# Two-pass products for the half-filled block of an MLP's width, in an fp32 kernel built from three-pass matmuls

## The chip, the cores and the metric

The kernel runs on one core of a Trainium2 chip. TensorE (PE; its weight loads are PEld) multiplies from SBUF into eight PSUM banks; VectorE (DVE) and ScalarE (ACT) read PSUM and SBUF; GpSimd (POOL) issues DMAs and does small copies and fills; SyncE (SP) issues DMAs. Each of them works through its own queue in order, and semaphores hold an instruction until what it needs is done. The metric is the time of one execution on the device, in microseconds.

## The reference

```python
xn = layernorm(x)                                              # x: 2048 tokens x 640 channels
a, b = xn @ hid_re.T, xn @ hid_im.T
fnet = seq_re @ a - seq_im @ b                                 # 2048 x 2048 matrices
h = layernorm(xn)
u = gelu(einsum("bsd,sf->bdf", h, w1) + b1)                    # F = 1728
mlp = einsum("bdf,fs->bds", u, w2) + b2                        # transposed to tokens x channels
return x + fnet + mlp
```

All arrays are fp32. The MLP runs over the tokens: the first product ("up") sums over 2048 tokens and gives 1728 rows, the second ("down") sums over these 1728 and gives 2048 rows, both 640 columns wide.

## The kernel before

**Three passes.** An fp32 operand is cut into a high and a low part (type fp32r): ScalarE rounds it (`high`, L132), VectorE subtracts (`low`, L135). `three` (L141) multiplies high x high, high x low and low x high into one bank: three matmuls, lines L144, L145 and L146 of the profile. Low x low is left out.

**Seven products.** Large products are done two block rows at a time (a row pair) by a scheme of Strassen's kind: a 2 x 2 block matrix A11, A12, A21, A22 of weights, times 2 x 2 blocks of the moving operand, in seven products P1, P5, P6, P2, P7, P3, P4 (in this order, `order` in `row_steps`, L701) instead of eight. The moving operand's seven sums and differences are made once (`moving_of`, L594) and stay in SBUF, high and low; each has 320 columns. For the weights, VectorE makes, for each row pair, s = A21 + A22, then A21 := A11 - A21, A11 := s - A11, and A12 := A12 - A11 (`sums_of`). P1 takes the old A11, P5 takes s, P6 the new A11, P2 the old A12, P7 the new A21, P3 the new A12, P4 takes A22. Seven products are seven steps; a step's weights are a *piece*.

**The stages.** After the Fourier part's products over the tokens and over the channels come four stages of this kind:

- up 0 and up 1: each sums over half of the tokens (four quarters q of 128 per block), in seven row pairs r = 0 to 6. Pair r holds the blocks r and r + 7 of the 1728 rows. Block 13 has only 64 rows (`TAIL`); the host fills it with a second copy of them. Up 0 puts its results into a DRAM tensor `up`; up 1 gets them back with an accumulating DMA (L804), adds bias and applies GELU (L809).
- down 0 and down 1: the sums over the blocks 0 to 3 with 7 to 10, and 4 to 6 with 11 to 13 (three quarters q). Each has eight row pairs of the 2048 rows; results are accumulated onto the output by POOL's DMAs (`collect`, L783). In the second half of block 13 the moving operand is zero (L814).

A step of the up stages and of down 0 is 4 x 3 matmuls, one of down 1 is 3 x 3, all of 128 x 320.

**The order.** `turn_of` (L931) writes each turn: DMA loads; reads of the PSUM bank of the last step; sums of the weights; the high part of the piece for the step three turns on; jobs (making the moving operands); the low part of that piece; then the matmuls of this turn's step. Four places for pieces take turns, so a high part waits for the matmuls of four steps before. The banks are handed out in turn: P1, P6, P7 and P4 add into bank "z", P5 and P3 into "y", P2 into "w". After each product the bank is read: the first time copied by ScalarE (L767), later added to SBUF by VectorE (L761). In up 1 the reads of P2 and P7 go *aside* (L825): ScalarE copies, and a DMA of POOL's accumulates onto `up`, before L804 reads it back.

Of the kernel before, what the change touches and what calls it, by code (L numbers as in the profile page):

```python
# [8 lines left out]
F32 = mybir.dt.float32  # L9
# [5 lines left out]
P = 128  # L15
# [51 lines left out]
def fnet_plus_mixer(  # L67
# [70 lines left out]
    def sub(to, a, b):  # L138
        nc.vector.tensor_sub(to, a, b)  # L139

    def three(psum, w, m, first, last):  # L141

        (wh, wl), (mh, ml) = w, m
        nc.tensor.matmul(psum, wh, mh, start=first, stop=False, skip_group_check=True)  # L144
        nc.tensor.matmul(psum, wh, ml, start=False, stop=False, skip_group_check=True)  # L145
        nc.tensor.matmul(psum, wl, mh, start=False, stop=last, skip_group_check=True)  # L146
# [14 lines left out]
    def cut_place(j, n):  # L161

        if n > CH:
            turn, width = (j - s_hid) % 3, 2 * n
        else:
            turn, width = (j - s_hid if j < s_hid else j - s_up + 3) % 4, 2 * CH
        return cut[:, turn * width : turn * width + 2 * n].rearrange("p (a n) -> p a n", a=2)

    def cut_piece(source, n):
# [12 lines left out]

        return top, bottom
# [515 lines left out]
        return raws[k][:, raw_turn[k], :n]  # L699

    def row_steps(  # L701
        stage, nq, load_piece, at, end, bias=(None, None), base=None, earliest=0, each=None, aside=None,
    ):


        s0, n = len(steps), nq * P
        raw, banks, held = {}, {}, {}

        def load(*names):
            for name in names:  # L710
                raw[name] = raw_slot(n)
                load_piece(raw[name], int(name[1]) - 1, int(name[2]) - 1)

        def first_sum():
            k = n if n == D else CH
            raw["s"] = raws[k][:, raws[k].shape[1] - 1, :n]
            nc.vector.tensor_add(raw["s"], raw["A21"], raw["A22"])
# [10 lines left out]
        sums_of = (  # L728
            first_sum, lambda: sub(raw["A21"], raw["A11"], raw["A21"]),
            lambda: sub(raw["A11"], raw["s"], raw["A11"]), lambda: sub(raw["A12"], raw["A12"], raw["A11"]),  # L730
        )
        bank_of = {1: "z", 6: "z", 7: "z", 4: "z", 5: "y", 3: "y", 2: "w"}
        of_moving = {1: 0, 2: 1, 3: 2, 5: 3, 7: 4, 4: 5, 6: 6}

        goes_to = {1: (0, 0, True), 5: (1, 1, True), 6: (0, 1, True), 2: (0, 0, False), 7: (1, 1, False),
                   3: (0, 1, False), 4: (1, 0, True)}

        def products(i):
            def run(w):
                if i in (1, 5, 2):  # L740
                    banks[bank_of[i]] = bank()
                for q in range(nq):
                    ks = slice(q * P, (q + 1) * P)
                    m = moving[stage, q]
                    three(
                        banks[bank_of[i]][:, :H2], (w[0][:, ks], w[1][:, ks]),
                        (m[:, 0, of_moving[i], :], m[:, 1, of_moving[i], :]), i in (1, 5, 2) and q == 0, q == nq - 1,
                    )
            return run

        def read(i):
            def run():
                if i == 1:
                    held["c"] = place[at]()
                row, half, fresh = goes_to[i]
                cols = slice(half * H2, (half + 1) * H2)
                c, b = held["c"][:, row, cols], banks[bank_of[i]][:, :H2]
                if aside and i in (2, 7):
                    aside(i, row, half, b)
                elif not fresh:  # L760
                    nc.vector.tensor_add(c, b, c)  # L761
                elif base:
                    nc.vector.tensor_add(c, b, base()[:, row, cols])  # L763
                elif bias[row] is not None:
                    nc.scalar.activation(c, b, AF.Identity, bias=bias[row])
                else:
                    nc.scalar.activation(c, b, AF.Copy)  # L767
# [4 lines left out]
            return run  # L772

        for e, names in loads_of.items():
            loads[max(s0 + e, earliest)].append(lambda names=names: load(*names))
        for e, f in zip(sums_at, sums_of):
            sums[s0 + e].append(f)
        for e, i in enumerate(order):
            steps.append(cut_piece(lambda i=i: raw[operand[i]], n) + (products(i),))
            reads[s0 + e + 1].append(read(i))  # L780
        return s0

    def collect(c, ts):  # L783
# [10 lines left out]
        return row_steps("hid", ND, load_piece, ("ca", "cb")[n % 2], lambda c: collect(c, ts), earliest=earliest)  # L794

    def up(stage, r, at):
        def load_piece(to, i, j):
            nc.sync.dma_start(to, w1[r + NF2 * i, 2 * stage + j])

        def end(c):  # L800
            if stage == 0:
                nc.gpsimd.dma_start(part_up[r], c)
                return
            nc.gpsimd.dma_start(c, part_up[r], accum_op=ALU.add)  # L804

            def gelu(i):
                f = r + NF2 * i
                rows = P if f < NF else TAIL
                nc.scalar.activation(  # L809
                    c[:rows, i, :], c[:rows, i, :], AF.Gelu_apprx_tanh, bias=b1_sb[:rows, f : f + 1]  # L810
                )
                if rows < P:

                    nc.gpsimd.memset(c[rows:, i, :], 0.0)  # L814


            e = s0 + 7
            timed[e + 6].append(lambda: gelu(0))
            timed[e + 6].append(lambda: gelu(1))
            if r < 4:  # L820
                timed[e + 8].append(lambda: jobs.extend(moving_of("down0", r, f"slab{4 + r}", lambda: c)))
            else:
                timed[e + 8].append(lambda: nc.gpsimd.dma_start(part_up[r], c))

        def aside(i, row, half, b):  # L825

            t = place["x1"]()[:, r % 2, i // 7 * H2 : (i // 7 + 1) * H2]
            nc.scalar.activation(t, b, AF.Copy)
            nc.gpsimd.dma_start(part_up[r][:, row, half * H2 : (half + 1) * H2], t, accum_op=ALU.add)

        s0 = row_steps(
            f"up{stage}", 4, load_piece, at, end, earliest=s_up - 4, aside=aside if stage else None,
        )
        return s0

    def down(stage, t, at):
        f0, nq = (0, 4) if stage == 0 else (4, 3)
        ts = (t, t + NS // 2)
        last = stage == 1 and t == NS // 2 - 1

        def load_piece(to, i, j):
            f = f0 + NF2 * j
            nc.sync.dma_start(to, w2[ts[i], :, f * P : (f + nq) * P])

        def each(c, row, half, whole):
            if whole:
                nc.sync.dma_start(out_rows[ts[row]][:, half * H2 : (half + 1) * H2], c)

        held = []

        def before():

            held.append(place["v"]())
            for i in range(2):
                nc.sync.dma_start(held[0][:, i, :], out_rows[ts[i]])

        if last:
            loads[len(steps) - LOADS].append(before)
        bias = [b2_sb[:, i : i + 1] if stage == 0 else None for i in ts]
        return row_steps(  # L860
            f"down{stage}", nq, load_piece, at, lambda c: collect(c, ts), bias, (lambda: held[0]) if last else None,
            each=each if last else None,
        )


# [49 lines left out]
    timed[s_down + 14].append(lambda: jobs.extend(rests_hid[0] + [gets_hid[2]] + rests_hid[1] + rests_hid[2]))  # L915
    for t in range(NS // 2):
        down(1, t, ("ca", "cb")[t % 2])

# [87 lines left out]
```

## Time and profile before

| | us |
|---|---|
| three runs | 878.43, 878.82, 878.82 (median 878.82) |
| the profiled execution | 878.46 |
| its span, first to last instruction | 876.5 |
| up 0 / up 1 (about) | 529 to 614 / 614 to 700.2 |
| down 0 / down 1 (about) | 700.2 to 798.7 / 798.7 to 872.5 |

The span is from the first instruction to the last; the execution's own time is 2.0 us longer. Times within a trace count from the span's start. A row of the timeline is start, duration, engine, line, operation, tile written <- tiles read, shape; in brackets stands the idle time before it and what ended it. Matmuls overlap, so their rate is read from starts and not from durations. VectorE's and ScalarE's instructions overlap a little too: 512 columns take 0.68 us and follow each other every 0.60 us.

### The profile page before, as it was taken

The page shows a single profiled execution, that of the slowest core. Times are in us where ns is not written, and L with a number is a line of the kernel's source. Part 1 is how long each engine was busy: PE and PEld are TensorE (multiplying, and loading weights), DVE is VectorE, ACT ScalarE, POOL GpSimd, SP SyncE. Part 2 cuts the span into 40 slices and gives each one's busy share as a digit, 9 for nine tenths or more (in the row PEclk, how much of TensorE's full clock was granted, in tenths as well). Part 3 has the DMA queues.
Part 4 walks back from the last instruction along what each step waited for, and adds up shares of the span by engine and source line. Part 5 has one row for each costly group of instructions (what it writes and reads, how often), then busy time and mean ns, then how long its engine had stood idle before and what let it go on. Part 6 is the DMA issues. An engine that isn't in the chain of part 4 may idle for free.

```text
span 876.5 us, 13992 instructions
## 1 busy us (share of the span) xinstructions
PE 871.5 (99%) x4957; PEld 798.5 (91%) x4957; DVE 705.5 (80%) x1183; ACT 524.8 (60%) x956; POOL 123.3 (14%) x166
## 2 busy tenths in 40 slices
PE   9999999999999999999999999999999999999998
PEld 6888888888888888889999999999999999999998
DVE  7878878785888888587887788898689878886775
ACT  6656575754656555557555546675587756655553
POOL 0110100101121111122101101000112211111111
PEclk9999999999999999999999999999999999999999
DMA  7781644529294646769766765544677896756876
GB/s 272 229 291 49 213 195 149 212 84 346 38 252 62 191 88 162 178 99 205 165 138 150 155 176 159 192 146 150 147 153 169 196 276 139 179 126 131 161 160 129
DMA packets 85685, 147.14 MB, mean 168 GB/s; under 512 B 8432, under 2 KB 35568, under 8 KB 85360
## 3 DMA queue, kind: packets, MB, share of 16 engines
q1 hardware_dynamic: 64848, 95.56, 33.6%
q0 software_dynamic: 20624, 50.54, 29.8%
q8 instruction: 39, 0.64, 0.3%
q14 instruction: 30, 0.25, 0.1%
q10 hardware_dynamic: 144, 0.16, 0.1%
HBM read 99.63 MB, written 51.84 MB: 173 GB/s over the span
## 4 chain that ended last, share of the span: by engine, by line
PE 99%; DMA 0%; ACT 0%; DVE 0%; SPq 0%; issue 0%
PE psum L144 31%; PE psum L146 31%; PE psum L145 31%; PE psum L444 6%; DMA pieces<-in_dft_seq 0%; ACT piece L133 0%; ACT n L236 0%; DVE pair L763 0%; SPq L468 0%; DVE r L205 0%; DVE norm L209 0%; DVE r L203 0%; ACT q L197 0%; DVE norm L212 0%
## 5 line engine op out<-in xcount | busy, mean ns | idle before, releaser
L136 DVE TENSOR_TENSOR piece<-pieces,piece 128x512 fp32r<-128x512 f32 (+2 forms) x508 | 347.4, 688 | 132.8 <-ACT piece L133 127.7
L133 ACT ACTIVATE piece<-pieces 128x512 fp32r<-128x512 f32 (+2 forms) x508 | 317.3, 628 | 210.3 <-PE psum L146 71.9
L144 PE MATMUL psum<-piece,n 128*128 128x512 f32 x504 | 196.1, 389 | 0.0
L145 PE MATMUL psum<-piece,n 128*128 128x512 f32 x504 | 196.1, 389 | 0.0
L146 PE MATMUL psum<-piece,n 128*128 128x512 f32 x504 | 196.1, 389 | 0.0
L144 PE MATMUL psum<-sup,piece 128*128 128x320 f32 x392 | 121.1, 309 | 0.0
L145 PE MATMUL psum<-sup,piece 128*128 128x320 f32 x392 | 121.1, 309 | 0.0
L146 PE MATMUL psum<-sup,piece 128*128 128x320 f32 x392 | 121.1, 309 | 0.0
L144 PE MATMUL psum<-sdown,piece 128*128 128x320 f32 x392 | 121.1, 309 | 0.0
L145 PE MATMUL psum<-sdown,piece 128*128 128x320 f32 x392 | 121.1, 309 | 0.0
L146 PE MATMUL psum<-sdown,piece 128*128 128x320 f32 x392 | 121.1, 309 | 0.0
L139 DVE TENSOR_TENSOR pieces<-pieces 128x512 f32<-128x512 f32 (+3 forms) x142 | 112.3, 791 | 1.9
L145 PEld LDWEIGHTS psum<-piece,n 128*128 128x128 f32 x504 | 94.6, 188 | 19.8
L146 PEld LDWEIGHTS psum<-piece,n 128*128 128x128 f32 x504 | 94.6, 188 | 19.7
L144 PEld LDWEIGHTS psum<-piece,n 128*128 128x128 f32 x504 | 94.6, 188 | 19.5
L146 PE MATMUL psum<-shid,piece 128*128 128x320 f32 x280 | 86.5, 309 | 0.0
L144 PE MATMUL psum<-shid,piece 128*128 128x320 f32 x280 | 86.5, 309 | 0.0
L145 PE MATMUL psum<-shid,piece 128*128 128x320 f32 x280 | 86.5, 309 | 0.0
L767 ACT ACTIVATE pair<-psum 128x320 f32<-128x320 f32 x104 | 45.4, 437 | 64.3 <-PE psum L146 63.5
L146 PEld LDWEIGHTS psum<-sdown,piece 128*128 128x128 f32 x392 | 73.6, 188 | 0.0
L144 PEld LDWEIGHTS psum<-sup,piece 128*128 128x128 f32 x392 | 73.6, 188 | 0.0
L145 PEld LDWEIGHTS psum<-sup,piece 128*128 128x128 f32 x392 | 73.6, 188 | 0.0
(98 smaller groups left out, 1108.8 us busy)
## 6 DMA issues: line engine op xcount, KB each, us to landing
pieces<-in_dft_seq SPq DMA_DIRECT2D x128, 256.0 KB, 4.9
pieces<-in_w SPq DMA_DIRECT2D x88, 256.0 KB, 3.6
y<-c POOLq DMA_DIRECT2D x84, 256.0 KB, 6.1
out<-pair POOLq DMA_DIRECT2D x38, 320.0 KB, 4.3
pieces<-y SPq DMA_DIRECT2D x32, 320.0 KB, 3.6
pieces<-in_w SPq DMA_DIRECT2D x32, 192.0 KB, 3.2
out<-in_x SPq DMA_DIRECT2D x16, 320.0 KB, 6.8
up<-pair POOLq DMA_DIRECT2D x8, 640.0 KB, 3.2
```

The costliest lines, as they stand in the source:

```text
L133: nc.scalar.activation(hi, src, AF.Copy)
L136: nc.vector.tensor_sub(lo, src, hi.bitcast(F32))
L139: nc.vector.tensor_sub(to, a, b)
L144: nc.tensor.matmul(psum, wh, mh, start=first, stop=False, skip_group_check=True)
L145: nc.tensor.matmul(psum, wh, ml, start=False, stop=False, skip_group_check=True)
L146: nc.tensor.matmul(psum, wl, mh, start=False, stop=last, skip_group_check=True)
L444: nc.tensor.matmul(banks[m, j], channels(k, j)[rows], w[cols], start=n == 0 and k == begin, stop=n == 2 and k == end, skip_group_check=True,)
L767: nc.scalar.activation(c, b, AF.Copy)
```

## The change

Three things, all where block 13 with its 64 rows takes part:

1. **Hi beside lo (up 0 and up 1, r = 6: P5, P7, P4).** Of s, A21 and A22 only 64 of 128 weight columns in each quarter are valid. `cut_halves` puts the 64 high columns beside their 64 low ones, and `pair_of` multiplies that with the moving high and the moving low part: two matmuls for three. The bank then holds the products of the high weights in partitions 0 to 63 and those of the low weights in 64 to 127; `read_short` adds the two halves. The bank of P7 is a new one ("t"), P3 goes to "z", P4 begins "y" anew. P7 is no longer read aside in up 1. POOL zeroes the invalid columns of s (`none`). The sums of A21 and the cuts take 256 columns instead of 512. The result goes out and comes back in two DMAs (128 x 640 and 64 x 640).
2. **Hi above lo (down 1: P2, P4).** There the last quarter of A12 and A22 has 64 valid rows of the sum and 64 that are the second copy. `cut_stacked` keeps the high part in partitions 0 to 63 and puts the low part into 64 to 127; the moving operand of that quarter gets its upper half copied into its lower half (`doubled`, two ScalarE jobs, 64 x 2 x 320 each). Two matmuls for three in that quarter.
3. **The first sum in down 1** is made in parts: VectorE 128 x 256 and 64 x 128, POOL copies A21's lower half of the last quarter (64 x 128).

With the two-pass products low x low is computed too.

```diff
+    def pair_of(w, m):
+        return lambda psum, first, last: [
+            nc.tensor.matmul(psum, w, m[i], start=first and i == 0, stop=last and i == 1, skip_group_check=True)
+            for i in range(2)
+        ]
+    def cut_halves(source):
...
+        def bottom():
+            a = held["piece"]
+            low(a[:, :, 1, :], parts(source()), a[:, :, 0, :])
+            return a.rearrange("p q a f -> p (q a f)")
+    def cut_stacked(source, n):
...
+        def bottom():
+            hi, lo = (held["piece"][:, i, :n] for i in range(2))
+            low(lo[:, : n - P], source()[:, : n - P], hi[:, : n - P])
+            below = hi[TAIL:, n - P :]
+            low(below, source()[TAIL:, n - P :], below)
+            return hi, lo
...
         def first_sum():
+            if stacked:
+                m = n - P
+                nc.vector.tensor_add(raw["s"][:, :m], raw["A21"][:, :m], raw["A22"][:, :m])
+                nc.vector.tensor_add(raw["s"][:TAIL, m:], raw["A21"][:TAIL, m:], raw["A22"][:TAIL, m:])
+                nc.gpsimd.tensor_copy(raw["s"][TAIL:, m:], raw["A21"][TAIL:, m:])
+                return
+            nc.vector.tensor_add(valid(raw["s"]), valid(raw["A21"]), valid(raw["A22"]))
...
+        if short:
+            bank_of |= {3: "z", 7: "t", 4: "y"}
+            begins = (1, 5, 2, 7, 4)
...
+                    if short and i in (5, 7, 4):
+                        pair_of(w[:, ks], m)(to, first, last)
+                    elif stacked and i in (2, 4) and last:
+                        pair_of(w[0][:, ks], m)(to, first, last)
+                    else:
+                        three(to, (w[0][:, ks], w[1][:, ks]), m, first, last)
...
+        def read_short(i):
...
+                elif i == 5:
+                    nc.scalar.activation(c22, below, AF.Copy)
+                    nc.vector.tensor_add(c22, above, c22)
+                elif i == 6:
+                    nc.scalar.activation(c21, above, AF.Copy)
...
+                elif i == 3:
+                    nc.scalar.activation(c12[TAIL:], below, AF.Copy)
+                    nc.vector.tensor_add(c12[:TAIL], above, c22)
+                    nc.vector.tensor_add(c22, c22, c21)
+                else:
+                    nc.vector.tensor_add(c21, above, c21)
+                    nc.vector.tensor_add(c21, below, c21)
...
+        if short:
+            sums[s0 - 6].append(none)
...
+    def doubled(i):
+        m = moving["down1", 2]
+        high(m[TAIL:, :, i, :], m[:TAIL, :, i, :].bitcast(F32))
```

**TensorE, up 1, r = 6, P5.** `sup` is the moving operand (a number for each quarter), `piece` the weights, `psum` the bank. Before, its four quarters:

```order
L144 MATMUL psum_98<-sup_4414,piece 128x320
L145 MATMUL psum_98<-sup_4414,piece 128x320
L146 MATMUL psum_98<-sup_4414,piece 128x320
L144 MATMUL psum_98<-sup_4611,piece 128x320
L145 MATMUL psum_98<-sup_4611,piece 128x320
L146 MATMUL psum_98<-sup_4611,piece 128x320
L144 MATMUL psum_98<-sup_4826,piece 128x320
L145 MATMUL psum_98<-sup_4826,piece 128x320
L146 MATMUL psum_98<-sup_4826,piece 128x320
L144 MATMUL psum_98<-sup_4970,piece 128x320
L145 MATMUL psum_98<-sup_4970,piece 128x320
L146 MATMUL psum_98<-sup_4970,piece 128x320
```

And now (L172 is `pair_of`; the last three rows are P6's first quarter):

```order
L172 MATMUL psum_99<-sup_4414,piece 128x320 x2
L172 MATMUL psum_99<-sup_4611,piece 128x320 x2
L172 MATMUL psum_99<-sup_4826,piece 128x320 x2
L172 MATMUL psum_99<-sup_4970,piece 128x320 x2
L144 MATMUL psum_98<-sup_4414,piece 128x320
L145 MATMUL psum_98<-sup_4414,piece 128x320
L146 MATMUL psum_98<-sup_4414,piece 128x320
```

Twelve matmuls are eight; the number of rows of the moving operand and its columns stay.

**VectorE, end of up 1, r = 6.** Rows L136 are low halves, L139 and L717 sums of the next stage's weights, L761 reads of PSUM. Before, from the low halves of P4 and of the next stage's first step on:

```order
L136 TENSOR_TENSOR piece<-pieces_120,piece 128x512 x2
L139 TENSOR_TENSOR pieces_120<-pieces_120 128x512
L136 TENSOR_TENSOR piece<-pieces_120,piece 128x512
L761 TENSOR_TENSOR pair<-psum_98,pair 128x320
L136 TENSOR_TENSOR piece<-pieces_120,piece 128x512 x2
```

And now from the same place (L861 to L865 are in `read_short`: P7's two adds, P3's two, P4's two):

```order
L136 TENSOR_TENSOR piece<-pieces_120,piece 128x4x64
L136 TENSOR_TENSOR piece<-pieces_120,piece 128x512
L864 TENSOR_TENSOR pair<-psum_101,pair 64x320
L865 TENSOR_TENSOR pair<-psum_101,pair 64x320
L139 TENSOR_TENSOR pieces_120<-pieces_120 128x512
L136 TENSOR_TENSOR piece<-pieces_120,piece 128x512
L861 TENSOR_TENSOR pair<-psum_98,pair 64x320
L862 TENSOR_TENSOR pair<-pair 64x320
L136 TENSOR_TENSOR piece<-pieces_120,piece 128x512
L864 TENSOR_TENSOR pair<-psum_99,pair 64x320
L865 TENSOR_TENSOR pair<-psum_99,pair 64x320
L136 TENSOR_TENSOR piece<-pieces_120,piece 128x512
```

One read has become six between the same low halves.

**VectorE, one row pair of down 1.** Before, from the first sum (L717) to the read of P2:

```order
L717 TENSOR_TENSOR pieces_120<-pieces_120 128x384
L136 TENSOR_TENSOR piece<-pieces_120,piece 128x384
L139 TENSOR_TENSOR pieces_120<-pieces_120 128x384
L136 TENSOR_TENSOR piece<-pieces_120,piece 128x384
L761 TENSOR_TENSOR pair<-psum_101,pair 128x320
```

And now (POOL's COPY stands in its own queue behind the two output DMAs of the row pair before; the L139 row is the first that waits for it):

```order
L764 TENSOR_TENSOR pieces_120<-pieces_120 128x256
L765 TENSOR_TENSOR pieces_120<-pieces_120 64x128
L136 TENSOR_TENSOR piece<-pieces_120,piece 128x384
L139 TENSOR_TENSOR pieces_120<-pieces_120 128x384
L136 TENSOR_TENSOR piece<-pieces_120,piece 128x256
L136 TENSOR_TENSOR piece<-pieces_120,piece 64x128
L826 TENSOR_TENSOR pair<-psum_95,pair 128x320
```

The sum and P4's low half are in two parts each; nothing has changed places.

More of the change, by code (lines that the diff above doesn't have):

```diff
@@ L701, in row_steps @@
     def row_steps(
-        stage, nq, load_piece, at, end, bias=(None, None), base=None, earliest=0, each=None, aside=None,
+        stage, nq, load_piece, at, end, bias=(None, None), base=None, earliest=0, each=None, aside=None, short=False,
+        stacked=False,
     ):
@@ L739, in run @@
             def run(w):
-                if i in (1, 5, 2):
+                if i in begins and bank_of[i] not in banks:
                     banks[bank_of[i]] = bank()
@@ L743, in run @@
                     ks = slice(q * P, (q + 1) * P)
[L744 to L748, printed above, removed]
+                    m = [moving[stage, q][:, a, of_moving[i], :] for a in range(2)]
+                    to, first, last = banks[bank_of[i]][:, :H2], i in begins and q == 0, q == nq - 1
+                    if short and i in (5, 7, 4):
[4 more added lines that the diff above has]
+                        three(to, (w[0][:, ks], w[1][:, ks]), m, first, last)
             return run
@@ L778, in row_steps @@
         for e, i in enumerate(order):
-            steps.append(cut_piece(lambda i=i: raw[operand[i]], n) + (products(i),))
-            reads[s0 + e + 1].append(read(i))
+            source = lambda i=i: raw[operand[i]]
+            if short and i in (5, 7, 4):
+                piece = cut_halves(source)
+            elif stacked and i in (2, 4):
+                piece = cut_stacked(source, n)
+            else:
+                piece = cut_piece(source, n)
+            steps.append(piece + (products(i),))
+            reads[s0 + e + 1].append((read_short if short else read)(i))
         return s0
@@ L796, in up @@
     def up(stage, r, at):
+        short = r == NF2 - 1
         def load_piece(to, i, j):
@@ L832, in up @@
             f"up{stage}", 4, load_piece, at, end, earliest=s_up - 4, aside=aside if stage else None,
+            short=short,
         )
@@ L861, in down @@
             f"down{stage}", nq, load_piece, at, lambda c: collect(c, ts), bias, (lambda: held[0]) if last else None,
-            each=each if last else None,
+            each=each if last else None, stacked=stage == 1,
         )
```

52 lines of the change are left out of this document (47 added, 5 removed).

## The prediction

> **What bounds the kernel now.** I read the engine shares first, then the chain that ended last, then the stages, then single instructions.
>
> ```profile
> PE 871.5 (99%) x4957; PEld 798.5 (91%) x4957; DVE 705.5 (80%) x1183; ACT 524.8 (60%) x956; POOL 123.3 (14%) x166
> ...
> PE 99%; DMA 0%; ACT 0%; DVE 0%; SPq 0%; issue 0%
> ```
>
> ```profile
> 529.00:614.00 85.00, 85.00 (x582) 85.00 (x581) 75.92 (x127) 54.44 (x100) 3.73 (x7) 1.00 0.51 163
> 614.00:700.20 86.20, 86.20 (x590) 86.20 (x589) 70.66 (x112) 62.14 (x120) 18.28 (x22) 1.00 0.72 166
> 700.20:798.70 98.50, 98.50 (x674) 98.50 (x673) 79.53 (x133) 56.38 (x103) 15.25 (x19) 1.00 0.71 175
> 798.70:872.50 73.80, 73.80 (x505) 73.80 (x504) 54.07 (x109) 37.39 (x82) 12.94 (x16) 1.00 0.74 152
> ```
>
> The first fence has the busy times and the chain, the second the stages up 0, up 1, down 0 and down 1, each with its length and then the busy time of PE, PEld, DVE, ACT and POOL, the granted clock (1.00) and the DMA share. PE is busy for the whole of every stage and makes 99% of the chain. But a busy PE row alone doesn't show a full rate, so I look at starts (start, duration, engine):
>
> ```profile
> 689.63 0.31 PE L144 MATMUL psum<-sup,piece 128*128 128x320 f32 x1
> 689.77 0.31 PE L145 MATMUL psum<-sup,piece 128*128 128x320 f32 x1
> 689.92 0.31 PE L146 MATMUL psum<-sup,piece 128*128 128x320 f32 x1
> ...
> 691.39 0.31 PE L144 MATMUL psum<-sup,piece 128*128 128x320 f32 x1
> ```
>
> From 689.63 to 691.39 one product of the last pair, P5 of up 1, takes its 12 matmuls: 1.76 us, 146.7 ns each. The three kinds start at even distances, although L144 and L145 load the same weights twice. So no kind is cheaper than another, and 0.31 us is latency, not spacing. The matmuls are never late: TensorE is the bound, and time falls with their number as long as that stays so.
>
> **What goes.** In each up stage, P5, P7 and P4 of r = 6 issue 4 x 2 matmuls for 4 x 3: 12 fewer, 24 in both stages. In down 1, P2 and P4 issue two for three in their last quarter, 2 fewer per row pair, 16 in eight. Together 40 x 146.7 ns = **5.87 us**: 1.76 in each up stage, 0.29 per row pair of down 1.
>
> [...]
>
> **What is added, and what hides it.** The prices (line, engine, shapes, count, then busy us and mean ns):
>
> ```profile
> L761 DVE TENSOR_TENSOR pair<-psum,pair 128x320 f32<-128x320 f32 x85 | 41.4, 487 | 14.7 <-PE psum L146 13.7
> ...
> L809 ACT ACTIVATE pair<-pair,b_sb 128x640 f32<-128x640 f32 x7 | 5.4, 816 | 0.0
> ...
> L136 DVE TENSOR_TENSOR n<-pair,n 128x256 fp32r<-128x256 f32 x6 | 2.5, 418 | 0.0
> ...
> L136 DVE TENSOR_TENSOR n<-x,n 128x128 fp32r<-128x128 f32 x8 | 2.3, 284 | 0.0
> ...
> L809 ACT ACTIVATE pair<-pair,b_sb 64x640 f32<-64x640 f32 x1 | 0.8, 817 | 0.0
> ```
>
> Half the partitions save nothing (816 and 817 ns), so I price the 64 x 320 adds at the 487 ns of full ones. No row shows an operation that reads partitions 64 to 127 and writes 0 to 63; I bound it between 487 ns and double that, and take 487.
>
> *Up, r = 6.* VectorE gains adds: 8 for 3 in up 0; 7 for 1 in up 1, where P7 no longer goes aside. That is at most 6 x 0.49 = 2.9 us. It saves on three low halves and two sums, which take 256 columns for 512 (418 ns for the 0.68 us of the rows below): 5 x 0.27 = 1.3 us. Up 0 has 9 us of idle time (75.92 of 85.00). Up 1 is tight at its end, so I follow VectorE's queue there:
>
> ```profile
> 692.30 0.68 DVE L136 TENSOR_TENSOR piece<-pieces,piece 128x512 fp32r<-128x512 f32 x1
> 692.90 0.68 DVE L717 TENSOR_TENSOR pieces<-pieces 128x512 f32<-128x512 f32 x1
> 693.50 0.68 DVE L136 TENSOR_TENSOR piece<-pieces,piece 128x512 fp32r<-128x512 f32 x1
> ...
> 695.44 1.35 DVE L136 TENSOR_TENSOR piece<-pieces,piece 128x512 fp32r<-128x512 f32 x2
> ...
> 701.47 0.69 DVE L136 TENSOR_TENSOR piece<-pieces,piece 128x512 fp32r<-128x512 f32 x1 [1.59 <-ACT piece L133]
> ```
>
> These are the low halves of P7 (692.30), P3 (693.50) and P4 (695.44), on the clock of this run. Before, P1 starts at 687.87 (689.63 less 1.76). With short products 1.17 us long, P3 now starts at 687.87 + 3 x 1.76 + 2 x 1.17 = 695.49, and P4 at 697.25. P7's low half gets about 0.25 shorter and the read of P5 comes in with 0.41 (the queue's pitch), so P3's low half ends near 694.18 + 0.16 = 694.34: 1.15 us early. P4's ends near 696.0, 1.2 early. The later adds go into the 1.59 us of idle time before 701.47. No wait: 0. If every 64 x 320 add cost double, the pieces behind them would still come within about 0.2 us of their time.
>
> The other new edge is the PSUM bank z: P6 adds into it once P1 has been read.
>
> ```profile
> 689.83 0.44 ACT L767 ACTIVATE pair<-psum 128x320 f32<-128x320 f32 x1
> ```
>
> The read ends at 690.27. P6 began at 691.39 and now begins at 690.80: 0.53 us of cover left of 1.12. If ScalarE is later than that, each tenth costs a tenth.
>
> *The two transfers of r = 6.* POOL issues two accumulating loads for one, and GELU must find them landed:
>
> ```profile
> 695.84 0.85 POOL L829 DMA_DIRECT2D up<-pairs  x1 [3.60 <-ACT pairs L828]
> 697.60 0.84 POOL L829 DMA_DIRECT2D up<-pairs  x1 [0.91 <-ACT pairs L828]
> 704.29 0.87 POOL L804 DMA_DIRECT2D pair<-up  x1 [5.85 <-DVE piece L136]
> ...
> 711.09 0.63 POOL L814 MEMSET pair<- 64x640 f32 x1 [5.36 <-DMA pair<-up]
> ```
>
> ```profile
> 711.39 1.54 ACT L809 ACTIVATE pair<-pair,b_sb 128x640 f32<-128x640 f32 x2
> ```
>
> ```profile
> DMA to landing us min/median/max: 5.9/6.7/7.6
> ```
>
> POOL's rows are the asides of P2 and P7, the load that gets r = 6 back, and the fill behind it; then come ScalarE's GELU and the times from issue to landing of all seven such loads. The load landed at about 711.1, 0.3 us before GELU's turn, which now comes 1.76 us sooner, at 709.6. But the load was issued 6.7 us after P7's aside, which is gone; 6.7 us after P2's (0.59 sooner for the short P5) is 695.84 - 0.59 + 6.7 = 702.0. So the two loads go out near 702.0 and 702.6 and land, by the 6.7 us of the median, near 708.7 and 709.3. Hidden; if not, the pieces that ScalarE makes behind GELU are over 2 us ahead of their steps. The second store of up 0's r = 6 is one more issue of 0.87 us or less on POOL, which does 3.73 us of work in that stage: 0.
>
> *Down 1.* VectorE splits three operations of a row pair in two: 284 + 418 less the 0.56 us of the last row below, +0.15 each, +0.44 us per row pair, onto 54.07 / 8 = 6.76 us in a row pair that shrinks from 9.24 to 8.95. That still leaves 1.7 us idle. POOL gets a COPY of 64 x 128 behind two DMA issues:
>
> ```profile
> 826.47 0.31 PE L144 MATMUL psum<-sdown,piece 128*128 128x320 f32 x1
> ```
>
> ```profile
> 826.14 0.86 POOL L785 DMA_DIRECT2D out<-pair  x1 [7.14 <-DVE pair L761]
> 827.40 0.85 POOL L785 DMA_DIRECT2D out<-pair  x1 [0.40 <-ACT pair L767]
> ```
>
> ```profile
> 829.35 0.55 DVE L717 TENSOR_TENSOR pieces<-pieces 128x384 f32<-128x384 f32 x1
> ...
> 830.67 0.55 DVE L139 TENSOR_TENSOR pieces<-pieces 128x384 f32<-128x384 f32 x1
> 831.51 0.56 DVE L136 TENSOR_TENSOR piece<-pieces,piece 128x384 fp32r<-128x384 f32 x1 [0.29 <-ACT piece L133]
> ```
>
> P1 of a row pair starts at 826.47. Then come POOL's rows and VectorE's: the first sum, the A21 difference, and P4's low half. The issues end at 828.25; the first to wait for the COPY is the A21 difference at 830.67. That gives 2.4 us. No row shows a COPY on POOL; the MEMSET at 711.09, with five times the columns, took 0.63 us, so I bound it by 0.13 (a fifth) and 0.63, and take 0.63, the row as it stands. Hidden. ScalarE's two copies of `doubled` have 640 columns each, so 0.82 us by L809's row, among 42 us of its idle time in down 0 (56.38 busy of 98.50): hidden, 1.6 us without that cover. The POOL fills of s stand a step ahead of the sum, 256 columns, so 0.63 us or less each: 0.
>
> **Sum.** 878.46 us (the profiled execution, span 876.5 and 2.0 around it) - 5.87 = 872.6. That execution lies 0.36 below the median, 878.82, from which the sum is 872.95; I say **872.8**.
>
> **Rivals.**
>
> *A: r = 6 waits for VectorE or ScalarE in up 1.* For it: VectorE's rows from 692.30 on follow each other at the queue's pitch, and the cover of bank z halves to 0.53 us. Against it: margins of 1.15 us and more, and the 1.59 us of idle time behind. I let it take back up to the 1.76 us of that stage: 873.8 if half, 874.6 if all. Chance 0.12.
>
> *B: the COPY holds VectorE in all eight row pairs, and the kernel is slower.* In-order VectorE stands at the A21 difference while P4's low half (831.51 to 832.07) waits behind it. P4 would start at 834.24 (P1 at 826.47, five steps of 1.32 and one of 1.17), so VectorE may be held 2.2 us beyond the 2.4: the COPY must take over 4.6 us before PE waits, and over 4.6 + 5.87 / 8 = 5.3 us before all is lost. At 6 us it would be 878.8 - 5.9 + 8 x 1.4 = 884. That is nine times the MEMSET row. Chance 0.04.
>
> [...]
>
> [...]
>
> *C: the matmuls go, but the rest doesn't close up*, because the pair runs slower than two thirds of three. For it: each matmul keeps its own weight load (4957 of each), and PEld is busy throughout these stages. Against it: the even spacing of 0.147 us whether the weights repeat or not. If a pair took the 0.44 us of three: no change, 878.8. Chance 0.04.
>
> **How the numbers follow.** Forecast 0.80 (872.4 to 873.3, by the spread of the runs before), A 0.12, B 0.04, C 0.04. The range runs from 872.3 to 874.4, that is, through most of A. Less than 0.2% (1.76 us) a measurement of this kernel can hardly tell from no change; forecast and A lie beyond that: faster 0.92, same 0.04, slower 0.04.
>
> **What would show it.** Right: 40 matmuls fewer, 146.7 ns spacing in the pairs too, PE busy through all stages, ends of up 0, up 1 and down 1 earlier by 1.76, 3.52 and 5.87. A would show as a PE gap at P6, P3 or P4 of r = 6; B as a VectorE wait on POOL ahead of the A21 difference, and gaps once per row pair; C as spacing over 0.2 us in the pairs' rows. The forecast is wrong if PE has any gap over 0.5 us between 602 and 867.

## The result, and the profile after

The changed kernel takes **872.18 us** (median of 4 runs, 872.09 to 872.75) against 878.82 us before (878.43 to 878.92, 4 runs): a ratio of 0.9927 with a 95% interval of 0.9909 to 0.9944, that is 6.64 us less. The forecast was 872.8 us. The measured median lies 0.6 us below it and 0.12 us below the lower end of the range, 872.3. One run further down, of the kernel with twelve added copies, took 1069.28 us at a granted clock of 0.753; that kernel's figures leave it out.

The profile's page of the kernel after, busy times and chain:

```profile
PE 864.9 (99%) x4917; PEld 792.5 (91%) x4917; DVE 709.7 (82%) x1218; ACT 524.8 (60%) x957; POOL 126.7 (15%) x177
...
PE 99%; DMA 0%; ACT 0%; DVE 0%; SPq 0%; issue 0%
```

40 matmuls are gone (4957 before), VectorE has 4.2 us more work, POOL 3.4, and the chain is still PE alone. The four stages after, by windows (length, then PE, PEld, DVE, ACT, POOL, the granted clock, DMA share, GB/s):

```profile
529.00:612.20 83.20, 83.20 (x569) 83.20 (x568) 74.67 (x128) 54.07 (x101) 4.07 (x8) 1.00 0.53 167
612.20:696.70 84.50, 84.50 (x578) 84.50 (x577) 70.76 (x118) 59.99 (x118) 18.33 (x23) 1.00 0.73 167
696.70:795.20 98.50, 98.50 (x674) 98.50 (x673) 82.14 (x140) 59.15 (x106) 16.40 (x21) 1.00 0.71 172
795.20:866.70 71.50, 71.50 (x490) 71.50 (x488) 56.61 (x132) 37.33 (x82) 15.04 (x23) 1.00 0.77 157
```

PE's time equals the length of each window, and from the first matmul of up 0 to the last of down 1 no two starts lie more than 0.147 us apart. So no stage waits, and the gap over 0.5 us that would have shown the forecast wrong is nowhere. The two-pass product P5 of r = 6, PE's timeline in up 1:

```profile
687.76 0.31 PE L146 MATMUL psum<-sup,piece 128*128 128x320 f32 x1
687.91 1.34 PE L172 MATMUL psum<-sup,piece 128*128 128x320 f32 x8
689.08 0.31 PE L144 MATMUL psum<-sup,piece 128*128 128x320 f32 x1
```

From 687.91 to 689.08 eight matmuls take 1.17 us: 146.3 ns each, the spacing of the three-pass products.

Where the 6.33 us between the two profiled executions are, worked out from the starts of the first and last matmuls of the stages in both traces:

| us | before | after | difference |
|---|---|---|---|
| first matmul of up 0, from the span's start | 527.71 | 527.75 | +0.04 |
| up 0 and up 1 | 172.48 | 168.96 | -3.52 |
| down 0 and down 1, to the last matmul's start | 172.33 | 169.99 | -2.35 |
| last matmul's start to the span's end | 3.95 | 3.66 | -0.28 |
| execution less span | 1.99 | 1.77 | -0.22 |
| profiled execution | 878.46 | 872.13 | -6.33 |

The two middle rows are the forecast, 24 and 16 matmuls at 146.7 ns. The ends give another 0.50 us. The last 0.3 us of the 6.64 is where the profiled executions lie: 0.36 below the median before, 0.05 below it after.

The covers of r = 6 came out as forecast. ScalarE after, its reads of P1 and P5 of r = 6:

```profile
688.11 0.44 ACT L848 ACTIVATE pair<-psum 128x320 f32<-128x320 f32 x1
688.44 0.41 ACT L133 ACTIVATE piece<-pieces 128x256 fp32r<-128x256 f32 x1
689.28 0.43 ACT L850 ACTIVATE pair<-psum 64x320 f32<-64x320 f32 x1 [0.43 <-PE psum L172]
```

The read of P1 out of bank z ends at 688.55; P6 starts at 689.08. That is the cover of 0.53 us that the forecast named. VectorE after, from the low half of P3 on:

```profile
691.92 0.68 DVE L136 TENSOR_TENSOR piece<-pieces,piece 128x512 fp32r<-128x512 f32 x1
...
694.80 0.48 DVE L864 TENSOR_TENSOR pair<-psum,pair 64x320 f32<-64x320 f32 x1
695.31 0.49 DVE L865 TENSOR_TENSOR pair<-psum,pair 64x320 f32<-64x320 f32 x1
695.72 0.68 DVE L139 TENSOR_TENSOR pieces<-pieces 128x512 f32<-128x512 f32 x1
...
700.20 0.69 DVE L139 TENSOR_TENSOR pieces<-pieces 128x512 f32<-128x512 f32 x1
...
704.51 0.69 DVE L136 TENSOR_TENSOR piece<-pieces,piece 128x512 fp32r<-128x512 f32 x1
705.71 0.49 DVE L826 TENSOR_TENSOR pair<-psum,pair 128x320 f32<-128x320 f32 x1 [0.50 <-PE psum L146]
```

P3's low half ends at 692.60 and P3 starts at 693.77: 1.17 us of margin. VectorE has no row with an idle time in brackets from 691.92 to 704.51: the added adds have used up its slack, and its first wait stands only at 705.71. Keep this in mind for the experiments.

POOL after, the transfers of r = 6 and a COPY of down 1:

```profile
699.16 1.72 POOL L913 DMA_DIRECT2D pair<-up  x2 [4.78 <-DVE pair L864]
700.39 1.09 POOL L934 DMA_DIRECT2D up<-pairs  x1
701.52 0.62 POOL L925 MEMSET pair<- 64x640 f32 x1
...
823.04 0.85 POOL L890 DMA_DIRECT2D out<-pair  x1 [0.21 <-issue]
823.58 0.61 POOL L766 COPY pieces<-pieces 64x128 f32<-64x128 f32 x1
```

The two loads go out from 699.16 on, about a microsecond earlier than forecast (702.0 less 1.76 is 700.24). The aside of P2, issued at 693.53, had landed after 5.1 us, at 698.64, and not after the 6.7 us of the forecast; VectorE's add, which ends at 699.04, came last. The loads landed at 704.56 and 706.45, before GELU's turn at 707.91. The COPY takes 0.61 us and is done at 824.19.

### The profile page after: what moved, and what is told of

The parts are those of the page before. It is cut to its first block, busy times and chain, and to the rows that moved or that the text cites. A ratio compares the mean times of both kernels' runs of the same rounds, so it can differ in the third digit from the quotient of the medians.

```text
span 870.4 us, 13982 instructions
## 1 busy us (share of the span) xinstructions
PE 864.9 (99%) x4917; PEld 792.5 (91%) x4917; DVE 709.7 (82%) x1218; ACT 524.8 (60%) x957; POOL 126.7 (15%) x177
## 4 chain that ended last, share of the span: by engine, by line
PE 99%; DMA 0%; ACT 0%; DVE 0%; SPq 0%; issue 0%
PE psum L146 30%; PE psum L145 30%; PE psum L144 30%; PE psum L488 6%; PE psum L172 1%; DMA pieces<-in_dft_seq 0%; ACT piece L133 0%; ACT n L280 0%; DVE pair L828 0%; SPq L512 0%; DVE r L249 0%; ACT q L241 0%; DVE norm L253 0%; DVE r L247 0%; DVE norm L256 0%
## 5 line engine op out<-in xcount | busy, mean ns | idle before, releaser
L136 DVE TENSOR_TENSOR piece<-pieces,piece 128x512 fp32r<-128x512 f32 (+2 forms) x524 | 348.9, 670 | 122.1 <-ACT piece L133 117.9
L133 ACT ACTIVATE piece<-pieces 128x512 fp32r<-128x512 f32 (+3 forms) x508 | 315.9, 626 | 207.9 <-PE psum L146 75.7
L146 PE MATMUL psum<-piece,n 128*128 128x512 f32 x504 | 196.1, 389 | 0.0
L144 PE MATMUL psum<-sdown,piece 128*128 128x320 f32 x376 | 116.2, 309 | 0.0
L145 PE MATMUL psum<-sdown,piece 128*128 128x320 f32 x376 | 116.2, 309 | 0.0
L146 PE MATMUL psum<-sdown,piece 128*128 128x320 f32 x376 | 116.2, 309 | 0.0
L144 PE MATMUL psum<-sup,piece 128*128 128x320 f32 x368 | 113.7, 309 | 0.0
L145 PE MATMUL psum<-sup,piece 128*128 128x320 f32 x368 | 113.7, 309 | 0.0
L146 PE MATMUL psum<-sup,piece 128*128 128x320 f32 x368 | 113.7, 309 | 0.0
L139 DVE TENSOR_TENSOR pieces<-pieces 128x512 f32<-128x512 f32 (+3 forms) x142 | 112.0, 788 | 1.9
L146 PEld LDWEIGHTS psum<-piece,n 128*128 128x128 f32 x504 | 94.6, 188 | 19.6
L146 PE MATMUL psum<-shid,piece 128*128 128x320 f32 x280 | 86.6, 309 | 0.0
L832 ACT ACTIVATE pair<-psum 128x320 f32<-128x320 f32 x96 | 41.8, 436 | 57.6 <-PE psum L146 52.1
L144 PEld LDWEIGHTS psum<-sdown,piece 128*128 128x128 f32 x376 | 70.6, 188 | 0.0
L145 PEld LDWEIGHTS psum<-sdown,piece 128*128 128x128 f32 x376 | 70.6, 188 | 0.0
L146 PEld LDWEIGHTS psum<-sdown,piece 128*128 128x128 f32 x376 | 70.6, 188 | 0.0
```

The lines of the kernel that those rows point to most:

```text
L133: nc.scalar.activation(hi, src, AF.Copy)
L136: nc.vector.tensor_sub(lo, src, hi.bitcast(F32))
```

## The experiments

### One part at a time, and both again

The first kernel keeps only hi beside lo (the first diff), the second only hi above lo (the second diff); the third and fourth are the changed kernel and the one before once more.

```diff
-            each=each if last else None, stacked=stage == 1,
+            each=each if last else None, stacked=False,
...
-        lambda: jobs.extend(rests_hid[0] + [gets_hid[2]] + rests_hid[1] + rests_hid[2] + [lambda i=i: doubled(i) for i in (1, 5)])
+        lambda: jobs.extend(rests_hid[0] + [gets_hid[2]] + rests_hid[1] + rests_hid[2])
```

```diff
-        short = r == NF2 - 1
+        short = False
```

> Only hi beside lo (up 0 and up 1, r = 6); down 1 as before. Count theory (each matmul that goes is worth 146.7 ns and all that is added stays hidden): 24 matmuls fewer, 3.52 us less than before, about 875.3 by the median of before. Ends theory (the change also shortens the end of the program, after the last matmul, by about 0.3 us): 3.5 to 3.8 less, with the tail after the last matmul shorter than 3.9 us; but the last row pair is not touched here, so the tail should be as before under it too.

> Only hi above lo in down 1; the up stages as before. Count theory: 16 matmuls fewer, 2.35 us less than before, about 876.5. Ends theory: the last product is one of the shortened ones, so the tail shrinks with it: 2.6 to 3.0 us less, tail after the last matmul about 3.66 us.

> The changed kernel itself once more, beside the same runs of before. Count theory: 5.87 us less in the stages; the rest of the 6.64 us that the medians showed is scatter of the start and the end of the program, so the difference of the medians should fall nearer to 5.9 to 6.3. Ends theory: 6.3 to 6.7 again, in each round.

> The kernel before against itself: 0 difference, within 0.3 us. Shows how far the spans of one program, and the time around them, scatter from run to run. Count theory: the tail after the last matmul and the time around the span vary by 0.2 us or more here too. Ends theory: the tail stays at 3.9 us and the time around the span at 2.0 us.

| | median of 5 (4th: 11) | ratio, interval | up and down, from starts | tail | execution less span |
|---|---|---|---|---|---|
| hi beside lo | 875.03 | 0.9956, 0.9943 to 0.9968 | 341.29 (-3.52) | 4.01 | 1.82 |
| hi above lo | 875.88 | 0.9967, 0.9955 to 0.998 | 342.47 (-2.35) | 4.36 | 1.77 |
| both, again | 872.18 | 0.9926, 0.9913 to 0.994 | 338.95 (-5.87) | 3.67 | 1.77 |
| before, again | 878.76 | 0.9999, 0.9991 to 1.0008 | 344.81 (0) | 3.94 | 2.01 |

The stages shrink by the count of matmuls to 0.01 us, in each part and in their sum: no part gives anything back. That settles the main term. The surplus at the ends (0.5 us) comes again in the third kernel and not in the fourth, so it belongs to the kernel. But it is not the last product's doing. DVE's last read, the last DMA issue and its landing lie at the same distance from the last matmul in before and after. The tail differs by one idle stretch between the starts of two semaphore instructions of POOL in the closing barrier: 0.37 us in before and 0.08 in after. In the first kernel a gap of 0.37 us stands at another place of that barrier; in the second the last DMA landed later, and its profiled execution was its slowest of five. The time around the span is shorter in every changed kernel, 1.77 to 1.82 against 2.0. Why is left open; no instruction of the trace lies there.

### How much cover VectorE had left

VectorE gets copies behind its reads of P5, P7, P3 and P4 of r = 6 in up 1, one each and, with `range(3)`, three each. They are work alone: what they write POOL's fill overwrites.

```diff
+                if aside and i in (5, 7, 3, 4):
+                    for _ in range(1):
+                        nc.vector.tensor_copy(c[TAIL:, 1, :H2], below)
```

> The changed kernel with one more VectorE read of PSUM (64 x 320, into a part of the pair that is not used) behind each of the reads of P5, P7, P3 and P4 of r = 6 in up 1: 4 more, some 1.6 us of VectorE. In the changed kernel's trace the low halves behind them are 1.2 to 2.1 us ahead of TensorE. Cover theory (late VectorE costs nothing until these margins are used up, then one for one): the smallest margin left is about 0.4 us, so 0, time as the changed kernel (872.2). Rival (VectorE is already the bound at that place): 1.6 us more.

> The same with three more reads at each of the four places, 12 in all, some 4.9 us of VectorE. Cover theory: the margins of P6 and P2 of down 0's first row pair (1.9 and 2.1 us) are overrun by about 2.8 us; the stage up 0 to down 1 gets 2.0 to 3.2 us longer, 874.2 to 875.4, with gaps of TensorE at these two steps and none elsewhere. Rival (VectorE catches up in idle time of its own, rival A never mattered): under 0.5 us more. Rival (VectorE is the bound): 4.9 us more.

Measured: 873.39 us (873.33 to 873.52) and 877.70 us (877.44 to 878.33, nine runs); up and down together 340.15 and 344.38 us, that is +1.21 and +5.43. Both expectations were too low, and both results lie nearer to the rival that has VectorE as the bound (1.6 and 4.9). With twelve copies PE also loses time where no gap was expected: besides P6 and P2 of down 0's first row pair, at P3 and P4 of r = 6 (0.38 and 0.22 us), and at P5 and P7 of that row pair (1.29 and 0.40 us).

Eight more copies cost 4.22 us, 0.53 us each, which is a copy's own pitch in VectorE's queue. So beyond the cover every copy counts in full. The cover is read from how late VectorE is: its sum of the weights at 700.20 (L139 in VectorE's rows above) starts 2.77 us later with four copies and 6.99 us later with twelve, counted from the first matmul of up 0. Less the losses of 1.21 and 5.43, both give 1.56 us. (The two losses alone, with 0.53 us for each of the first four copies too, would give 0.9; but those cost 0.69 us each, because the rows beside them overlap less: the reads ahead of the four copies go on after 0.49 to 0.52 us and not 0.40 to 0.42.) I had taken the cover from the low halves of r = 6 (1.17 us and more) and the idle time behind. Where the loss of the first kernel arises, ScalarE's timeline of that kernel:

```profile
697.85 0.63 ACT L133 ACTIVATE piece<-pieces 128x512 fp32r<-128x512 f32 x1 [1.69 <-DVE pieces L139]
698.39 1.54 ACT L923 ACTIVATE pairs<-pairs,b_sb 128x640 f32<-128x640 f32 x2
699.83 0.62 ACT L133 ACTIVATE piece<-pieces 128x512 fp32r<-128x512 f32 x1
700.47 0.53 ACT L830 ACTIVATE pair<-psum,b_sb 128x320 f32<-128x320 f32 x1
```

and PE's, of the same kernel:

```profile
700.08 0.31 PE L146 MATMUL psum<-sdown,piece 128*128 128x320 f32 x1
701.05 0.42 PE L144 MATMUL psum<-sdown,piece 128*128 128x320 f32 x1 [0.67 <-ACT pair L830]
```

Beside it ScalarE in the changed kernel:

```profile
696.50 0.64 ACT L133 ACTIVATE piece<-pieces 128x512 fp32r<-128x512 f32 x1 [0.33 <-DVE pieces L139]
697.03 1.54 ACT L920 ACTIVATE pairs<-pairs,b_sb 128x640 f32<-128x640 f32 x2
698.47 0.62 ACT L133 ACTIVATE piece<-pieces 128x512 fp32r<-128x512 f32 x1
699.12 0.53 ACT L830 ACTIVATE pair<-psum,b_sb 128x320 f32<-128x320 f32 x1
...
702.19 0.53 ACT L830 ACTIVATE pair<-psum,b_sb 128x320 f32<-128x320 f32 x1 [0.57 <-PE psum L146]
```

The place is not in r = 6 but in the first row pair of down 0. A high part waits for VectorE's sum of the weights (L139, at 695.72 in the changed kernel). Behind it in ScalarE's queue stand the two GELUs of r = 5, then the read of P1 out of bank z, and P6 waits for that bank. In the changed kernel this read ends at 699.65 and P6 starts at 700.23: a cover of 0.58 us. With four copies the high part starts 1.35 us later, the read too, and PE stands still for 0.83 us. Another 0.18 us is lost at P7, and after each of the two gaps the next start comes a tenth late (0.26 us after 701.05 and 0.25 after 704.85, for 0.147).

### Was it GELU in front of the read?

If ScalarE's queue at that place is the cause, the two GELUs of r = 5 two turns later, behind the read, should take the loss away. Once with the four copies, once without.

```diff
-            timed[e + 6].append(lambda: gelu(0))
-            timed[e + 6].append(lambda: gelu(1))
+            timed[e + (8 if r == NF2 - 2 else 6)].append(lambda: gelu(0))
+            timed[e + (8 if r == NF2 - 2 else 6)].append(lambda: gelu(1))
```

> The kernel of the four added VectorE copies, with the two GELUs of row pair 5 of up 1 placed two turns later, so that ScalarE reads P1 of the first row pair of down 0 before it runs them. Theory (the loss went through ScalarE's queue: VectorE's sum A11 makes ScalarE's piece 1.35 us late, GELU's 1.54 us stand between that piece and the read of P1 out of bank z, and P6 waits for the bank): with GELU behind the read the read ends 1.5 us earlier, the gap of 0.83 us ahead of P6 is gone, and up and down together take 338.95 us again, 872.2 in all; a remnant up to 0.3 us may be left where later reads now stand behind GELU. Rival (VectorE's delayed sums or low halves hold PE themselves): the gap stays, 340.15 us for the two products and 873.4 in all.

> The changed kernel with the same later place of the two GELUs, without the added copies: the control. Theory and rival both expect no change, 338.95 us for the two products and 872.2 in all; the cover of bank z ahead of P6 of the first row pair of down 0 grows from 0.58 us to about 2.1 us (0.58 + 1.54). If GELU two turns later is itself harmful, its loss shows here alone, and the run above is to be read less this loss.

Measured: 873.48 us (873.23 to 874.65) with the copies, 872.15 us (871.85 to 872.53) without. Without the copies up and down take 338.95 us, as expected, but the cover ahead of P6 grew to 1.03 us only and not to 2.1: the read now waits for P1's own matmuls. With the copies the gap of 0.83 us ahead of P6 is gone, yet up and down together take 340.15 us, to the nanosecond what they took with GELU in its old place. The theory's cure worked where it was applied and saved nothing. PE in the kernel with both, at P6, P2 and P7:

```profile
700.39 0.31 PE L145 MATMUL psum<-sdown,piece 128*128 128x320 f32 x1
700.71 0.42 PE L146 MATMUL psum<-sdown,piece 128*128 128x320 f32 x1
...
702.42 0.31 PE L145 MATMUL psum<-sdown,piece 128*128 128x320 f32 x1
703.00 0.42 PE L146 MATMUL psum<-sdown,piece 128*128 128x320 f32 x1 [0.27 <-DVE piece L136]
...
704.87 0.41 PE L144 MATMUL psum<-sdown,piece 128*128 128x320 f32 x1
```

and VectorE's low halves for the first two:

```profile
699.97 0.69 DVE L136 TENSOR_TENSOR piece<-pieces,piece 128x512 fp32r<-128x512 f32 x1
...
702.26 0.69 DVE L136 TENSOR_TENSOR piece<-pieces,piece 128x512 fp32r<-128x512 f32 x1
```

P6 and P2 begin without a wait, but their third matmul, the first that takes the low half (L146), starts only when VectorE has made it: the low halves end at 700.66 and 702.95, the matmuls start at 700.71 and 703.00. With the slower next start these two cost 0.28 and 0.54 us. The rest is lost at P7. ScalarE in the same kernel:

```profile
703.77 0.63 ACT L133 ACTIVATE piece<-pieces 128x512 fp32r<-128x512 f32 x1 [1.82 <-DVE pieces L139]
704.31 0.51 ACT L830 ACTIVATE pair<-psum,b_sb 128x320 f32<-128x320 f32 x1
```

and the first weight load of P7 (PEld):

```profile
704.87 0.19 PEld L144 LDWEIGHTS psum<-sdown,piece 128*128 128x128 f32 x1 [0.40 <-ACT pair L830]
```

P7 is the fifth product of down 0's first row pair. Its bank z comes free with the read of P6, at 704.82. That read stands behind a high part which waits 1.82 us for VectorE's next sum (L139 at 700.20 in the changed kernel, 702.99 here). In the changed kernel the read of P6 ends at 702.72 and P7 starts at 703.75, a cover of 1.03 us; the read is 2.1 us late here, so P7 starts 1.1 us late, and the restart of PE costs a further tenth (0.25 us from 704.87 to the next start, for 0.147). That is the whole loss, 1.21 us. What is lost before only shortens the wait at P7: the gaps at P6 and P2 here, and with GELU in its old place the 0.83 us ahead of P6. So the rival is right in the time, and at P6 and P2 in its mechanism too: VectorE's queue, late by four copies and with no idle time before 705, holds PE itself. At P7, which sets the total, the wait ran through ScalarE, in whose queue a bank's read stands behind a high part that waits for VectorE. That the last read sets the loss is read from the trace; no kernel was run that moves it.

### The COPY on POOL, five and twelve times

POOL repeats the COPY of each row pair of down 1, five times and, with `range(12)`, twelve times.

```diff
-                nc.gpsimd.tensor_copy(raw["s"][TAIL:, m:], raw["A21"][TAIL:, m:])
+                for _ in range(5):
+                    nc.gpsimd.tensor_copy(raw["s"][TAIL:, m:], raw["A21"][TAIL:, m:])
```

> POOL's COPY of 64 x 128 done five times over in each row pair of down 1 (about 3.0 us of POOL at 0.6 us each). By the changed kernel's trace TensorE waits only if the COPY takes over about 5 us (2.7 us until the A21 difference, and P4's low half then 2 us ahead). Cover theory: 0, 872.2; VectorE waits up to 0.4 us for POOL ahead of the A21 difference. [...]

> The same with twelve COPYs in each row pair (about 7.2 us at 0.6 us each). Cover theory: 2.2 us beyond the 5.0 in each of seven to eight row pairs, 15 to 18 us more (887 to 890), so slower than the kernel before; if the COPYs follow each other faster than 0.6 us, accordingly less (at 0.5 us: 8 us more). Rival (POOL's work is hidden whatever its length): 872.2.

Measured: 872.27 us (872.15 to 872.44) with five, up and down together 338.95, no change. With twelve 888.24 us (887.47 to 889.46), a ratio of 1.011 (1.0094 to 1.0127) to before, up and down together 354.14: 15.2 us more. VectorE's waits in the kernel with twelve (us in all, times, the longest):

```profile
DVE pieces L139 <- POOL pieces L767: 17.8, 8, 3.0
```

Eight waits, one per row pair, at the A21 difference, as rival B had it, and gaps in PE at P4 of seven row pairs. What PE waits for there, in the same form:

```profile
PE psum L144 <- DVE pair L827: 10.5, 7, 2.1
```

That is VectorE's read of P7, which frees bank z for P4 and stands in VectorE's queue behind the A21 difference and P4's low half. In the second row pair the COPYs take 5.56 us from 807.91 on, the difference starts at 813.50, P4's low half is done at 814.72 and the read of P7 at 816.10, and P4 starts at 816.25, 2.04 us late. So PE waits once the COPYs take more than about 3.5 us (5.56 less 2.04, an estimate), sooner than the 4.6 us of rival B and the 5.0 us that I expected. That the time still came out where I expected it is luck: a COPY took 0.41 us on the mean and not 0.6, the cover was smaller, and 3.0 of the 15.2 us are matmuls at a granted clock of 0.50 behind two of the gaps (last section).

The rival's mechanism exists; what it lacks in the changed kernel is size: there the COPY is done at 824.19, and the next A21 difference starts at 826.30. The COPY in its forms, groups by line and shape, of the kernel after,

```profile
L766 POOL COPY pieces<-pieces 64x128 f32<-64x128 f32 x8 | 4.9, 609 | 0.0
L764 DVE TENSOR_TENSOR pieces<-pieces 128x256 f32<-128x256 f32 x8 | 3.3, 417 | 0.0
L765 DVE TENSOR_TENSOR pieces<-pieces 64x128 f32<-64x128 f32 x8 | 2.2, 277 | 0.0
```

and of the kernel with five:

```profile
L767 POOL COPY pieces<-pieces 64x128 f32<-64x128 f32 x40 | 19.9, 498 | 2.0
L764 DVE TENSOR_TENSOR pieces<-pieces 128x256 f32<-128x256 f32 x8 | 4.1, 508 | 0.0
L765 DVE TENSOR_TENSOR pieces<-pieces 64x128 f32<-64x128 f32 x8 | 3.0, 371 | 0.0
```

The columns behind the bar are busy us, mean ns of one, and idle time before. VectorE's adds beside the COPYs are 0.09 us longer each.

## Why the prediction was right, and where it was off

- **What goes: 5.87 us.** Measured 5.867 (344.813 less 338.946), and -3.52 and -2.35 for the parts alone. The step "matmuls by their spacing" holds exactly, for pairs as for threes. Rival C (pairs run slower) is out: eight in 1.17 us.
- **What is added costs nothing.** The 64 x 320 adds were priced at 487 ns; they took 476 and 493 (L864, L865). An operation that reads partitions 64 to 127 and writes 0 to 63 is L865: it takes 17 ns longer than L864, and the queue goes on to it 0.51 us after L864 (694.80 to 695.31) and not 0.41. The COPY was priced at 0.63 and took 0.61, which is luck: the price was that of a fill of five times the columns, and a COPY with VectorE idle took 0.29 (last section). The three parts of VectorE in down 1 took 417, 277 and 291 ns for 418, 284 and 284.
- **The covers in r = 6.** P3 1.17 us for 1.15, P4 1.26 for 1.2, bank z 0.53 for 0.53. Rival A didn't come. The forecast's price for lateness ("each tenth costs a tenth") is what the copies showed, but with four of them one place further on: the forecast let the later adds go "into the 1.59 us of idle time before 701.47". That time is used up, and what was left, about 1.6 us, hangs on the low halves and bank reads of down 0's first row pair. With twelve copies gaps came at P3 and P4 of r = 6 too, where rival A had placed them. The forecast didn't look at down 0. It was no part of the time, but it is the margin that a further change would meet first.
- **The transfers.** Hidden, as forecast; the time of issue was 1 us too late in the forecast, since the aside landed after 5.1 us and not 6.7, and VectorE's add then held the loads for 0.4 us more. The fill behind them (L925) no longer waits for a transfer at all: before, it waited 5.36 us.
- **The sum.** The term that was mis-sized is the one the forecast didn't write: "span 876.5 and 2.0 around it" was carried over whole. Outside the stages the changed kernel is 0.50 us shorter (0.28 in the closing barrier, 0.22 around the span), which turns 872.6 into 872.13. The step from 872.6 to 872.8, half the way to the median, was scatter: after the change the profiled execution lies only 0.05 below its median. The choice of 872.8, and a range that began at 872.3, left no room below for that: the lower end came from the spread of the runs of one kernel, and the ends of a program differ by a few tenths from kernel to kernel (tails of 3.66 to 4.36 us, 1.77 to 2.01 us around the span).

## What to carry to other kernels

Where TensorE never waits, as in the four stages here, a change is worth its matmuls by their measured spacing (here 40 x 146.7 ns), and the rest of the work is only a question of cover. Follow that cover past the end of the stage, through every queue in order: the nearest limits here were in the next stage, a bank's read on ScalarE behind a part that waited for VectorE, and VectorE's own low halves. Known work added in two sizes shows what a further piece costs (0.53 us a copy); the cover is how late the queue got less what was lost (2.77 less 1.21 us). A wait that is cured at one place may come back whole at the next, as the 0.83 us ahead of P6 did (340.15 us with that gap and without it), so compare lengths and not gaps.

## What the runs showed of the hardware

*The granted clock behind two gaps.* In the kernel with twelve COPYs PE stands still seven times for 0.6 to 2.3 us. After two of them, of 2.04 and 2.28 us, the granted clock was 0.50 for 3.41 us, from 817.04 and from 851.17. These two starts lie 34.13 us apart, ten times 3.41. Windows of 3.41 us counted from these two starts (length and PE's busy time first; the last but two columns are the granted clock, DMA share and GB/s behind it):

```profile
803.39:806.80 3.41, 1.61 (x11) 1.64 (x12) 3.38 (x8) 0.69 (x2) 0.12 (x1) 1.00 0.36 115
813.63:817.04 3.41, 1.53 (x11) 1.29 (x10) 3.35 (x9) 0.75 (x2) 0.00 (x0) 1.00 0.41 131
817.04:820.45 3.41, 3.41 (x15) 3.41 (x14) 2.22 (x6) 1.02 (x3) 2.42 (x4) 0.50 0.47 49
834.10:837.52 3.42, 2.45 (x17) 2.19 (x15) 1.78 (x5) 0.95 (x2) 1.30 (x5) 1.00 0.46 131
847.76:851.17 3.41, 1.45 (x10) 1.48 (x11) 3.35 (x9) 0.53 (x2) 0.00 (x0) 1.00 0.37 119
868.24:871.65 3.41, 1.86 (x13) 1.59 (x11) 2.35 (x6) 0.53 (x1) 0.84 (x3) 1.00 0.65 235
```

From 817.3 to 820.5 matmuls started every 267 ns, which cost some 1.5 us on top of that gap, and as much after the other. After three other gaps of 2.0 us the clock stayed at 1.00. Those gaps are as long as the first of the two, but lie otherwise in such windows: PE was busy for 1.53 and 1.45 us of the windows ahead of the slow ones, and for 1.61, 1.86 and, with the gap split between two windows, 2.45 us of the others. So the gap's length alone doesn't tell the two kinds apart. What does was not shown: these are five gaps of one run.

*A COPY on POOL and VectorE's adds.* In the kernel with twelve, a COPY of 64 x 128 took 0.29 us, and 0.35 us from one to the next, while VectorE stood idle (the 2.66 us up to 813.50). In the kernel with five, the forty COPYs took 0.29 to 0.71 us, 0.51 at the median; five of them, from 814.96 on, took 2.54 us together with VectorE at work all the while, and the first of these lies partly under the row of a DMA issue (814.41 to 815.26). The 0.61 us of the changed kernel don't show whether VectorE or the DMA issue makes a COPY longer, since half of that COPY lies under the row of a DMA issue (823.04 to 823.89). VectorE's adds L764 and L765 took 0.51 and 0.37 us beside a queue of five COPYs, and 0.42 and 0.28 us in the changed kernel: 0.09 us longer per operation, a third of a COPY of 0.29 us. Why was not shown.

*The closing barrier* has a stretch of 0.37 us between two of POOL's semaphore instructions that comes in some kernels, at different places, and not in others; the time around the span is 2.0 or 1.8 us by kernel. Neither was explained.
